# RetNet attention and a SiLU MLP on one core: k and q of three more units transposed by DMA, and the w_out slices converted later

## The chip, the cores and the metric

The kernel runs on one core of one Trainium2 chip. The metric is the device time of one execution in microseconds; less is better. The time of the kernel before is the median of three runs.

## The reference

```python
# q, k, v: (B=4, H=8, S=768, D=64); w_in: (512, 2048); w_out: (2048, 512)
gamma = 1.0 - 2.0 ** (-5.0 - arange(H));  scale = 1.0 / sqrt(D)
for t in range(S):                                  # per batch and head
    state = gamma * state + outer(k[t], v[t])       # (D, D)
    y[t] = scale * (q[t] @ state)
x = y.transpose(0, 2, 1, 3).reshape(3072, 512)      # (B*S, H*D)
h = x @ w_in
out = (h * (1 / (1 + exp(-h)))) @ w_out             # (3072, 512)
```

The weights reach the kernel as 64-bit numbers, two 32-bit words for each element. The output is 32-bit.

## The kernel before, in words

**Chunks and units.** The 768 tokens of each batch are cut into 6 chunks (`NC`) of 128 tokens (`C`). A unit is one chunk of one batch, all 8 heads: 24 units, numbered with the batch running fastest, so that unit 14 is chunk 3, batch 2. The recurrence over tokens is replaced by matmuls within a chunk (scores of q and k times a decay mask) and a state carried from chunk to chunk.

**Precision.** The large products are done in three parts: an operand is split into a high part, a remainder and a mixed part, and the sum of the part products stands for the full precision. So one 512-wide product takes 12 matmuls: 8 into the PSUM bank `ha` (parts 0 and 1) and 4 into the bank `hb` (part 2).

**Phase 1** makes g = silu(x w_in) block by block. `product_in(c, f)` is the block of chunk c (4 batches x 128 tokens = 512 columns) and slice f (128 of the 2048 columns of w_in, `NF` = 16 slices). Its 12 matmuls are at L650. ScalarE copies `ha` out (L660), VectorE subtracts `hb` (L665, kept in `taken_out`), ScalarE applies silu (L670), and the block is stored to DRAM by a DMA on the SyncE queue (L676), one product later. `ha` and `hb` come from three PSUM banks taken in turn (`turn`, L370), which the transposes of k use as well. Blocks of g on chip have three buffers (`hpool`).

**Phase 2** reads g back (L689), splits it (L715 on ScalarE, L717 and L718 on VectorE) and multiplies by w_out (L967, L975); the outputs leave at L984 to L996.

**Visits.** Attention is laid between the products of phase 1. `visit(m)` does, for unit m, the transposes of k and q; for unit m-1, the state sums (L452) and the scores (L462) with their mask and state update on VectorE; for unit m-2, the output y (L501). Its matmuls stand between those of two products. Unit 14 is visited behind product (1,15), units 15, 16 and 17 behind (2,9), (2,11) and (2,13), and from then on one unit behind every fourth product of chunks 3 and 4: (3,1), (3,5) and so on.

**Two ways to transpose.** `FAR` = 17 parts them.

- Units under `FAR`: `stage_t` does 8 transposes on TensorE (L436), four of k into a bank of `turn` and four of q into bank `q`, and two copies on ScalarE take them out (L438).
- Units from `FAR` on: `part_t` copies k and q on GpSimd into two planes of 16 bits (L412), `turn_t` transposes the planes by DMA on the SyncE queue (L419), and `join_t` joins them again on ScalarE (L426). The copies are issued in the visit, the transposing DMAs one product later, the joins in the third product, well before the scores of that unit, which stand in the next visit.

**Slices of the weights.** A slice of w_in or w_out is loaded two takes ahead (`wf`, two buffers). Each `take_w` converts one slice from 64-bit words to 32-bit: one instruction on ScalarE (L196) and six on VectorE: L199, L202, L206, L209, L212, L217. The slices of w_out, 16 of them, go to DRAM again, from the buffer `cw`, of which there is one. In chunk 5 `w_out(f)` reads them back behind product (5, f) and splits them: L120 and L126 on ScalarE, L123 and L128 on VectorE.

**What sets the order.** TensorE's order is the order of the program. On the other engines a scheduler places the instructions, with rules laid over it: `queue(i)` puts what is issued under it right behind instruction i on its engine, `behind_copy` and `behind_next` hold work that goes right behind L660 and L665 of the next product. A list of products, `steps`, is walked from first to last; `takes` lists the products that a slice is converted behind:

```python
takes += [(0, NF - 2), (2, half), (2, half + 2), (2, half + 4)]
takes += [(3, f) for f in (0, 3, 7, 11, 14)]
takes += [(4, f) for f in (3, 7, 11, 14)]
takes += [(5, f) for f in (2, 5, 8)]
```

These sixteen entries (`NF` = 16, `half` = 8) are those of w_out; the earlier ones are those of w_in. A visit that is hung to a product stands in the dictionary `behind`.

**Buffers.** Tiles live in pools by tag: `kf`, `qf`, `vf` for loaded k, q and v (3, 2 and 3 buffers), `kt` (2) and `qt` (3) for transposed tiles, `cw` (1) for a converted slice. `late_y(b)` reads back four tiles of chunk 2 that had been parked in DRAM, into `kt` for even b and `qt` for odd b.

Of the kernel before, what the change touches and what calls it, by code (L numbers as in the profile page):

```python
# [13 lines left out]
FP32 = mybir.dt.float32  # L14
FP32R = mybir.dt.float32r
U32 = mybir.dt.uint32
U16 = mybir.dt.uint16
# [16 lines left out]
def kernel(  # L34
# [28 lines left out]
    nc = tc.nc  # L63
    B, H, S, D = q.shape
    DM, DF = moe_w_in.shape
    C = 128
    NC = S // C
    HP = H // 2
    KIN = DM // 128
    NF = DF // 128  # L70
# [10 lines left out]
    def pool(name, bufs, **kw):  # L81
        return ctx.enter_context(tc.tile_pool(name=name, bufs=bufs, **kw))
# [6 lines left out]
    one = pool("one", 1)  # L89
    hpool = pool("hpool", 3)  # L90
    stage = pool("stage", 2)
    conv = pool("conv", 1)
# [45 lines left out]
    units = [(c, b) for c in range(NC) for b in range(B)]  # L138
    kqv = {"k": {}, "q": {}, "v": {}}
    EARLY = 2 * B  # L140

    FAR = 4 * B + 1
    early = {}

    def load(name, n):
        if n >= len(units):
            return
        c, b = units[n]
        src = {"k": k, "q": q, "v": v}[name]
        if n < EARLY:  # L150

            if n not in early:
                early[n] = wpool.tile([128, 3, H, D], FP32, tag=f"w{4 + n}", name=f"kqv_{n}")
            t = early[n][:, "kqv".index(name)]
        else:
            t = ld.tile([128, H, D], FP32, tag=f"{name}f", name=f"{name}f_{n}",
                        bufs=2 if name == "q" else 3)
        nc.sync.dma_start(out=t, in_=src[b, :, ds(c * C, C)].rearrange("h t d -> t h d"))
        kqv[name][n] = t
# [87 lines left out]
    def queue(ins):  # L247

        return ExitStack() if written[0] or ins is None else tc.issue_after(ins)
# [104 lines left out]
    xt, kt, qt, am = {}, {}, {}, {}  # L354
    behind_next, behind_copy, half_split = [], [], []
    taken_out, copied, masked, fenced = [], [], [], []
# [25 lines left out]
    def scale_k(n):  # L382
        if 0 <= n < len(units):
            t = kqv["k"][n]
            if units[n][0] == NC - 1:
                t = t[:D]
            if 2 * B + 1 < n < 3 * B + 2:

                def half(heads):
                    for h in heads:  # L390
                        nc.scalar.activation(out=t[:, h, :], in_=t[:, h, :], func=AF.Copy,
                                             scale=gk[:, units[n][0], h : h + 1])

                half(range(H // 2))
                behind_copy.append(lambda: half(range(H // 2, H)))
                return
            g = gk[: t.shape[0], units[n][0], :].unsqueeze(2).to_broadcast([t.shape[0], H, D])
            nc.vector.tensor_tensor(out=t, in0=t, in1=g, op=ALU.mult)
# [5 lines left out]

    planes, turned = {}, {}

    def part_t(n):

        for name, (p, tag, bufs) in (("q", (ld, "kf", 3)), ("k", (one, "kt", 2))):
            src = kqv[name].pop(n) if name == "q" else kqv[name][n]  # L410
            t = p.tile([128, 2 * H * D], U16, tag=tag, name=f"{name}p_{n}", bufs=bufs)
            nc.gpsimd.tensor_copy(out=t.rearrange("p (w h d) -> p w h d", w=2, h=H),  # L412
                                  in_=src.bitcast(U16).rearrange("p h (d w) -> p w h d", w=2))
            planes[name, n] = t

    def turn_t(n):
        for name, (p, tag, bufs) in (("q", (ld, "qf", 2)), ("k", (one, "qt", 3))):
            t = p.tile([128, 2 * HP, C], U16, tag=tag, name=f"{name}w_{n}", bufs=bufs)
            nc.sync.dma_start_transpose(out=t, in_=planes.pop((name, n)))  # L419
            turned[name, n] = t  # L420

    def join_t(name, n):

        to, bufs = (qt, 3) if name == "q" else (kt, 2)
        to[n] = one.tile([128, HP, C], FP32, tag=f"{name}t", name=f"{name}t_{n}", bufs=bufs)
        nc.scalar.copy(out=to[n].bitcast(U16).rearrange("p a (t w) -> p w a t", w=2),  # L426
                       in_=turned.pop((name, n)).rearrange("p (w a) t -> p w a t", w=2))

    def stage_t(n):

        for name, to, bufs, src, tp in (
                ("kt", kt, 2, kqv["k"][n], turn(f"kp_{n}")),
                ("qt", qt, 3, kqv["q"].pop(n), banks("q", f"qp_{n}", 1)[:, 0])):
            tp = tp.rearrange("p (a t) -> p a t", a=HP)
            for a in range(HP):
                nc.tensor.transpose(tp[:, a, :], src[:, 2 * a : 2 * a + 2, :], ident)  # L436
            to[n] = one.tile([128, HP, C], FP32, tag=name, name=f"{name}_{n}", bufs=bufs)
            evac[:] = [nc.scalar.copy(out=to[n], in_=tp).ins]  # L438
# [88 lines left out]
    def finish_y(n, yp):  # L527
        list(steps_y(n, yp))
# [52 lines left out]
    y_late = {}  # L581

    def late_y(b):
        tag = ("kt", "qt")[b % 2]
        y_late[b] = one.tile([128, KIN, C], FP32, tag=tag, name=f"yr_{b}", bufs=2 + b % 2)
        nc.sync.dma_start(out=y_late[b], in_=y_dram[b])

    def late_x(b):
# [9 lines left out]
    def halves(m):  # L598

        first, mid, last = (0 <= m - i < len(units) for i in range(3))  # L600
        if first and m < FAR:
            stage_t(m)
        if last:
            scores, states_with, yp = stage_y(m - 2)
            scores()
            states_with(0)
        yield
        if mid:
            sc, sums = score_tile(m - 1)
            stage_s(m - 1, sums)  # L610
            stage_a(m - 1, sc)
            if 1 < m <= 3 * B + 1 and units[m - 1][1] == 0:
                next_chunk()

            with queue(taken_out[0]) if m > 3 * B + 1 else ExitStack():
                finish_a(m - 1, sc, sums)
            scale_q(m - 1)
            if m > 3 * B + 1 and units[m - 1][1] == B - 1:

                behind_copy.append(next_chunk)  # L620
        if first and m < FAR:
            scale_k(m)
        if last:
            states_with(1)
            finish_y(m - 2, yp)

        if FAR <= m < len(units):
            with queue(fenced[0]):
                part_t(m)
        for name in "kqv":  # L630
            for n in (m + 1, m + 2):
                if n >= EARLY and n == (m + 1 if name == "v" or n > FAR else m + 2):
                    load(name, n)
        if EARLY + 2 <= m < 3 * B + 2:
            with queue(masked[0]):
                end_w()
                if m != 3 * B:
                    begin_w()


    pending = []

    def product_in(c, f):
# [168 lines left out]
    def KA(n):  # L812
        t = kqv["k"][n]
        for h in range(H):
# [73 lines left out]
    half = NF // 2  # L888
# [7 lines left out]
    steps = pairs + three + rest + last + groups  # L896
    takes = [(1, 5)] + [(0, f) for f in range(6, half)]
    takes += [(2, half - 4), (2, half - 2)]
    takes += [(0, half), (0, half + 3), (1, half + 1), (1, half + 3)]
    takes += [(0, NF - 2), (2, half), (2, half + 2), (2, half + 4)]  # L900
    takes += [(3, f) for f in (0, 3, 7, 11, 14)]
    takes += [(4, f) for f in (3, 7, 11, 14)]
    takes += [(5, f) for f in (2, 5, 8)]
    behind = {x: lambda: next(half_visits) for x in pairs[:-1]}
    behind[pairs[-1]] = lambda: [visit(3 * B + 1), behind_next.append(end_w)]
    at = ([(1, NF - 1)] + [(2, f) for f in range(NF - 7, NF - 2, 2)] +
          [(c, 4 * i + 1) for c in range(3, NC - 1) for i in range(B)])
    for i, x in enumerate(at):
# [4 lines left out]
    behind[1, NF - 1] = lambda: [late_x(3), visit(EARLY + 6)]  # L913


    far = {steps.index(x): EARLY + 6 + i for i, x in enumerate(at)
           if FAR <= EARLY + 6 + i < len(units)}
    for n, (c, f) in enumerate(steps):
        if n - 2 in far:
            behind_next.append(lambda m=far[n - 2]: scale_k(m))  # L920
        if n - 3 in far:
            behind_copy.append(lambda m=far[n - 3]: [join_t(name, m) for name in "qk"])
        product_in(c, f)
        put_g(1)
        store_w()
        if (c, f) in takes:
            take_w(taken_out[0], n < len(pairs + three))
        behind.get((c, f), lambda: None)()
        if n - 1 in far:
            turn_t(far[n - 1])  # L930
        if c == NC - 1:
            if f == 0:
                for i in range(W_READ):
                    get_w(i)
            if f < NF - 4:
                w_out(f)
            if f >= NF - 6:
                if f == NF - 6:
                    for n in range(G_AHEAD):
                        get(n)  # L940
                if f >= NF - S_AHEAD:
                    split(f - NF + S_AHEAD)
    put_g(0)

    for c in range(NC):
# [9 lines left out]
        for f in range(NF):  # L955
            n = c * NF + f
# [3 lines left out]
            t = ready[n]  # L960
# [17 lines left out]
        for b in range(B):  # L978
            oa, ob = acc[b]
            o = one.tile([128, DM], FP32, tag=("kt", "qt")[b % 2], name=f"o_{c}_{b}",  # L980
                         bufs=(2, 3)[b % 2])
# [8 lines left out]
            n = 2 if b == B - 1 else 1  # L990
# [36 lines left out]
```

## Time and profile before

| | before |
|---|---|
| median of three runs | 621.68 us (620.67, 621.68, 622.66) |
| profiled execution | 619.42 us, its span 617.6 us |
| granted TensorE clock, mean | 1.000 |
| VectorE busy | 422.9 us |
| ScalarE busy | 313.0 us |
| GpSimd busy | 22.6 us |
| DMA | 107.31 MB, mean 174 GB/s |

Busy time is what the engine's instructions occupy, and overlapping instructions make it longer than what they hold the engine for; so for TensorE the chain of waits is the better measure. In the names of engines, PE is TensorE, DVE VectorE, ACT ScalarE, POOL GpSimd and SP SyncE. `L650` is line 650 of the kernel.

One wait on the page is peculiar to this kernel: `POOL token L377`. It comes from `fence`, a tiny memset on GpSimd by which half of the y matmuls of a visit are held until the other half is done.

### The profile page before, as it was taken

The numbers are of one execution on the slowest core, as the hardware profiler recorded it, in microseconds if no ns is written. First come the engines' busy times: TensorE is split into PE (matmuls) and PEld (weight loads), VectorE is DVE, ScalarE is ACT, GpSimd is POOL, SyncE is SP. The second block draws the span as 40 slices with busy tenths as digits, with TensorE's granted clock in tenths as the row PEclk, the third lists the DMA queues.
The fourth block names the chain that finished last, engine by engine and source line by source line (L and its number), as shares of the span: only waits on it lengthen the run. The fifth ranks groups of instructions, "written<-read, shape, count | busy, mean of one in ns | idle before, by whom it ended". The sixth has DMA issues, their size and how long they took to land.

```text
span 617.6 us, 13494 instructions
## 1 busy us (share of the span) xinstructions
PE 603.8 (98%) x5384; PEld 497.5 (81%) x5384; DVE 422.9 (68%) x731; ACT 313.0 (51%) x595; POOL 22.6 (4%) x79
## 2 busy tenths in 40 slices
PE   6899999999999999999999999999999999999997
PEld 5777887888888888888788888888888888888886
DVE  4998889899789877676699773635545453654631
ACT  6678896676654667766587732312221221412311
POOL 3000000000001111120000000000000000000000
PEclk9999999999999999999999999999999999999999
DMA  9989896464677999989767542533524433442301
GB/s 191 225 203 228 243 240 200 157 198 157 222 177 208 259 255 239 259 223 282 255 230 248 203 139 68 171 102 100 173 69 134 140 103 102 141 132 89 116 1 68
DMA packets 137999, 107.31 MB, mean 174 GB/s; under 512 B 94801, under 2 KB 103249, under 8 KB 137937
## 3 DMA queue, kind: packets, MB, share of 16 engines
q1 hardware_dynamic: 135056, 101.21, 57.5%
q10 hardware_dynamic: 2880, 5.24, 2.3%
q8 instruction: 42, 0.69, 0.5%
q14 instruction: 21, 0.16, 0.1%
HBM read 66.06 MB, written 36.70 MB: 166 GB/s over the span
## 4 chain that ended last, share of the span: by engine, by line
PE 84%; DVE 0%; DVEq 0%; issue 0%; POOLq 0%
PE ha L650 25%; PE o L967 21%; PE oa L967 14%; PE hb L650 12%; PE ob L967 7%; PE y L501 2%; PE sc L462 1%; PE sc L452 1%; PE o L975 0%; PE oa L975 0%; PE qp L436 0%; PE kp L436 0%; PE ob L975 0%; DVE o L993 0%; DVEq L1022 0%
## 5 line engine op out<-in xcount | busy, mean ns | idle before, releaser
L650 PE MATMUL ha<-xt,wi 128*128 128x512 f32 x768 | 193.8, 394 | 1.3 <-ACT xt L557 0.7
L650 PEld LDWEIGHTS ha<-xt,wi 128*128 128x128 f32 x768 | 141.9, 188 | 33.6 <-ACT wi L126 1.2
L967 PE MATMUL o<-wo,gs 128*128 128x512 f32 x564 | 143.2, 389 | 0.0
L717 DVE TENSOR_TENSOR gs<-gr,gs 128x512 fp32r<-128x512 f32 x96 | 62.1, 685 | 90.3 <-ACT gs L715 90.3
L967 PEld LDWEIGHTS o<-wo,gs 128*128 128x128 f32 x564 | 105.9, 188 | 21.9
L715 ACT ACTIVATE gs<-gr 128x512 fp32r<-128x512 f32 x96 | 53.6, 621 | 134.2 <-issue 131.8
L967 PE MATMUL oa<-wo,gs 128*128 128x512 f32 x376 | 115.8, 389 | 0.0
L650 PE MATMUL hb<-xt,wi 128*128 128x512 f32 x384 | 102.9, 390 | 0.0
L665 DVE TENSOR_TENSOR g<-g,hb 128x512 f32<-128x512 f32 x96 | 65.6, 683 | 42.0 <-ACT g L660 26.3
L650 PEld LDWEIGHTS hb<-xt,wi 128*128 128x128 f32 x384 | 71.8, 188 | 15.5 <-DVE g L665 0.2
L670 ACT ACTIVATE g<-g 128x512 f32<-128x512 f32 x96 | 60.3, 628 | 47.1 <-DVE g L665 47.1
L967 PEld LDWEIGHTS oa<-wo,gs 128*128 128x128 f32 x376 | 70.6, 188 | 14.7
L967 PE MATMUL ob<-wo,gs 128*128 128x512 f32 x188 | 73.7, 392 | 0.0
L660 ACT ACTIVATE g<-ha 128x512 f32<-128x512 f32 x96 | 57.0, 594 | 31.9 <-PE ha L650 15.1
L718 DVE SCALAR_TENSOR_TENSOR gs<-gs 128x512 fp32r<-128x512 f32 x96 | 62.0, 683 | 0.0
L967 PEld LDWEIGHTS ob<-wo,gs 128*128 128x128 f32 x188 | 35.3, 188 | 8.7 <-DVE o L985 1.6
L196 ACT ACTIVATE ca<-wf 128x512 f32<-128x512 f32 x32 | 21.4, 668 | 6.0 <-DVE cw L217 5.5
L212 DVE SCALAR_TENSOR_TENSOR ca<-wf,ca 128x512 f32<-128x512 uint32 x32 | 22.7, 710 | 0.5
L984 ACT ACTIVATE o<-o 128x512 f32<-128x512 f32 x10 | 6.0, 600 | 33.4 <-PE o L967 33.0
L206 DVE SCALAR_TENSOR_TENSOR cs<-ca,cs 128x512 uint32<-128x512 uint32 x32 | 22.1, 691 | 0.9
L501 PE MATMUL y<-qt,mid 64*64 64x64 f32 x384 | 20.2, 224 | 1.0 <-POOL token L377 1.0
L470 DVE TENSOR_TENSOR am<-sc,decay 128x512 f32<-128x512 f32 x24 | 16.5, 687 | 6.6 <-PE sc L462 6.5
(93 smaller groups left out, 562.0 us busy)
## 6 DMA issues: line engine op xcount, KB each, us to landing
gd<-g SPq DMA_DIRECT2D x96, 256.0 KB, 3.1
gr<-gd SPq DMA_DIRECT2D x96, 256.0 KB, 2.7
wf<-in_moe_w_out_dram SPq DMA_DIRECT2D x16, 512.0 KB, 4.2
out_dram<-o ACTq DMA_DIRECT2D x20, 256.0 KB, 2.1
wf<-in_moe_w_in_dram SPq DMA_DIRECT2D x16, 256.0 KB, 4.2
wf<-in_moe_w_in_dram SPq DMA_DIRECT2D x32, 128.0 KB, 4.0
kf<-in_k_dram SPq DMA_DIRECT2D x16, 256.0 KB, 5.1
qf<-in_q_dram SPq DMA_DIRECT2D x16, 256.0 KB, 4.0
```

What stands on the lines that cost most here:

```text
L196: nc.scalar.activation(out=a.bitcast(FP32), in_=hi.bitcast(FP32), func=AF.Abs, scale=65536.0)
L206: nc.vector.scalar_tensor_tensor(out=s, in0=a, scalar=3, in1=s, op0=ALU.logical_shift_left, op1=ALU.bitwise_or)
L212: nc.vector.scalar_tensor_tensor(out=p.bitcast(FP32), in0=lo, scalar=2.0 ** -52, in1=p.bitcast(FP32), op0=ALU.mult, op1=ALU.mult)
L501: i = nc.tensor.matmul(yp[ts(e, D), o, a, :], lhsT=lhsT, rhs=rhs, start=(e, o) not in started, stop=True, skip_group_check=True).ins
L650: nc.tensor.matmul(hb if i == 2 else ha, lhsT=w_sb[f][:, i, ts(kk, 128)], rhs=xt[c][:, i, kk, :], start=kk == 0 and i != 1, stop=kk == KIN ...
L660: copied[:] = [nc.scalar.activation(out=hs, in_=ha, func=AF.Copy, scale=ONE_E).ins]
L665: taken_out[:] = [nc.vector.tensor_tensor(out=hs, in0=hs, in1=hb, op=ALU.subtract).ins]
L670: nc.scalar.activation(out=hs, in_=hs, func=AF.Silu)
L715: nc.scalar.activation(out=t[:, 0, :], in_=g, func=AF.Copy, scale=HALF)
L717: nc.vector.tensor_tensor(out=t[:, 1, :], in0=g, in1=high, op=ALU.subtract)
L718: nc.vector.scalar_tensor_tensor(out=t[:, 2, :], in0=t[:, 1, :].bitcast(FP32), scalar=-1.0 / EPS, in1=high, op0=ALU.mult, op1=ALU.add)
L967: nc.tensor.matmul(o, lhsT=g, rhs=wo[f][:, i, :], start=f == 0 and i != 1, stop=f == NF - 1 and i != 0)
```

## The change

`FAR` goes from 17 to 14: k and q of units 14, 15 and 16 go the way of the DMA as well, and TensorE no longer transposes them. A second bound, `LATER` = 17, keeps what units from 17 on do as it was. What belongs to it:

- Unit 14 is split long ahead: its `part_t` is tied to L665 of product (2,3), its transposes follow behind (2,5), its join behind L660 of (2,8). Unit 15 is split in the visit of 14, turned behind (2,8) and joined at (2,10); unit 16 is split in the visit of 15, turned behind (2,10) and joined at (2,12).
- Loads: k and q of 15 and q of 16 are loaded at hand-set places, and k of 16 into the buffer `cw`.
- `late_y` of odd batches uses `cw` instead of `qt`, whose buffers now carry planes.
- As `cw` is used by these, no slice of w_out can be converted there before the end of chunk 2. The takes at (0,14), (2,8), (2,10) and (2,12) fall away, and (2,15), one more in chunk 3, one more in chunk 4 and one more in chunk 5 come instead.

```diff
-    FAR = 4 * B + 1
+    FAR = 3 * B + 2
+    LATER = 4 * B + 1
...
+        if n == LATER - 1 and name == "k":
+            t = conv.tile([128, H, D], FP32, tag="cw", name=f"kf_{n}")
+            nc.sync.dma_start(out=t, in_=src[b, :, ds(c * C, C)].rearrange("h t d -> t h d"))
+            kqv[name][n] = t
+            return
...
-    def part_t(n):
+    def part_t(n, after=None):
...
+            if after is not None:
+                tc.add_manual_dep(i, after.name, mybir.DependencyInfo(
+                    mybir.DependencyClass.Sync, mybir.DependencyReason.DATA), reason="later")
...
-        tag = ("kt", "qt")[b % 2]
-        y_late[b] = one.tile([128, KIN, C], FP32, tag=tag, name=f"yr_{b}", bufs=2 + b % 2)
+        p, tag, bufs = ((one, "kt", 2), (conv, "cw", 1))[b % 2]
+        y_late[b] = p.tile([128, KIN, C], FP32, tag=tag, name=f"yr_{b}", bufs=bufs)
...
-        if first and m < FAR:
+        if first and m < LATER:
             scale_k(m)
...
-        if FAR <= m < len(units):
+        n = m if m >= LATER else m + 1
+        if FAR < n < len(units) and (m < LATER - 1 or m >= LATER):
             with queue(fenced[0]):
-                part_t(m)
+                part_t(n)
...
-    takes += [(0, NF - 2), (2, half), (2, half + 2), (2, half + 4)]
-    takes += [(3, f) for f in (0, 3, 7, 11, 14)]
-    takes += [(4, f) for f in (3, 7, 11, 14)]
-    takes += [(5, f) for f in (2, 5, 8)]
+    takes += [(2, NF - 1)]
+    takes += [(3, f) for f in (0, 3, 6, 8, 11, 14)]
+    takes += [(4, f) for f in (0, 3, 7, 11, 14)]
+    takes += [(5, f) for f in (1, 3, 5, 8)]
...
+    first_far = steps.index((2, 3))
+    parts = {first_far: FAR}
+    turns_at = {first_far + 2: FAR, far[FAR] + 1: FAR + 1, far[FAR + 1] + 1: FAR + 2}
+    joins_at = {far[m] + 1: m for m in range(FAR, LATER)}
+    for m in range(LATER, len(units)):
+        turns_at[far[m] + 1], joins_at[far[m] + 3] = m, m
+    scales_at = {far[m] + 2: m for m in range(LATER, len(units))}
+    loads_at = {first_far + 4: [("k", FAR + 1), ("q", FAR + 1)], far[FAR] + 1: [("q", FAR + 2)]}
```

More of the change, by code (lines that the diff above doesn't have):

```diff
@@ L411, in part_t @@
             t = p.tile([128, 2 * H * D], U16, tag=tag, name=f"{name}p_{n}", bufs=bufs)
-            nc.gpsimd.tensor_copy(out=t.rearrange("p (w h d) -> p w h d", w=2, h=H),
-                                  in_=src.bitcast(U16).rearrange("p h (d w) -> p w h d", w=2))
+            i = nc.gpsimd.tensor_copy(
+                out=t.rearrange("p (w h d) -> p w h d", w=2, h=H),
+                in_=src.bitcast(U16).rearrange("p h (d w) -> p w h d", w=2)).ins
+            if after is not None:
+                tc.add_manual_dep(i, after.name, mybir.DependencyInfo(
+                    mybir.DependencyClass.Sync, mybir.DependencyReason.DATA), reason="later")
             planes[name, n] = t
@@ L625, in halves @@
             finish_y(m - 2, yp)
-        if FAR <= m < len(units):
+        n = m if m >= LATER else m + 1
+        if FAR < n < len(units) and (m < LATER - 1 or m >= LATER):
             with queue(fenced[0]):
-                part_t(m)
+                part_t(n)
         for name in "kqv":
             for n in (m + 1, m + 2):
-                if n >= EARLY and n == (m + 1 if name == "v" or n > FAR else m + 2):
+                if (n, name) not in apart and n >= EARLY and n == (
+                        m + 1 if name == "v" or n >= LATER else m + 2):
                     load(name, n)
@@ L638, in halves @@
                     begin_w()
+    apart = [(FAR + 1, "k"), (FAR + 1, "q"), (FAR + 2, "q")]
     pending = []
@@ L913 @@
     behind[1, NF - 1] = lambda: [late_x(3), visit(EARLY + 6)]
-    far = {steps.index(x): EARLY + 6 + i for i, x in enumerate(at)
-           if FAR <= EARLY + 6 + i < len(units)}
-    for n, (c, f) in enumerate(steps):
[L919 to L922, printed above, removed]
+    far = {m: steps.index(x) for m, x in enumerate(at, EARLY + 6)}
+    first_far = steps.index((2, 3))
[6 more added lines that the diff above has]
+    loads_at = {first_far + 4: [("k", FAR + 1), ("q", FAR + 1)], far[FAR] + 1: [("q", FAR + 2)]}
+    for n, (c, f) in enumerate(steps):
+        if n in scales_at:
+            behind_next.append(lambda m=scales_at[n]: scale_k(m))
+        if n in joins_at:
+            behind_copy.append(lambda m=joins_at[n]: [join_t(name, m) for name in "qk"])
+        if n in parts:
+            behind_next.append(lambda m=parts[n]: part_t(m, taken_out[0]))
         product_in(c, f)
@@ L928 @@
         behind.get((c, f), lambda: None)()
-        if n - 1 in far:
-            turn_t(far[n - 1])
+        if n in turns_at:
+            turn_t(turns_at[n])
+        for name, m in loads_at.get(n, ()):
+            load(name, m)
         if c == NC - 1:
```

## The prediction

> **What bounds the kernel now.** First the busy times and the slices of the page, then the chain that ended last around the transposes, then the busy time by stretch of chunk 5, and last the order of time on DVE there.
>
> ```profile
> PE 603.8 (98%) x5384; PEld 497.5 (81%) x5384; DVE 422.9 (68%) x731; ACT 313.0 (51%) x595; POOL 22.6 (4%) x79
> PE   6899999999999999999999999999999999999997
> ```
>
> PE is at 90% or more from the third slice (about 31 us) to the last but one. From 100 us to 600 us it is busy in every 25 us stretch but for 0.3 us at 302 us, so a microsecond of PE work removed there is a microsecond of the end, as long as nothing else takes its place. How long PE work really holds the engine must be read from the chain, because matmuls overlap:
>
> ```profile
> 169.41 0.91 PE hb L650 x4
> 170.32 0.44 PE kp L436 x4
> 170.76 0.44 PE qp L436 x4
> 171.19 0.86 PE y L501 x48
> 172.05 0.47 PE sc L452 x32
> 172.52 0.47 PE sc L462 x32
> 172.99 0.23 PE y L501 x16
> 173.22 2.04 PE ha L650 x8
> ...
> 196.02 0.86 PE y L501 x48
> 196.88 0.47 PE sc L452 x32
> 197.34 0.47 PE sc L462 x32
> 197.81 0.23 PE y L501 x16
> 198.04 2.04 PE ha L650 x8
> ```
>
> Columns: start, length, engine, tile, line. The visit of unit 14 (170.32 to 173.22) lasts 2.90 us, those of 15 and 16 (178.89, 187.45) the same; the visit of 17 (196.02 to 198.04), whose k and q already come by DMA, lasts 2.02. The difference is exactly the eight L436 transposes, 0.44 + 0.44.
>
> DVE, with 68%, looks free, but not where the slices of w_out are finished:
>
> ```profile
> 305.00:325.00 20.00, 20.00 (x90) 16.55 (x89) 19.26 (x35) 16.41 (x31) 0.00 (x0) 1.00 0.64 216
> 325.00:340.00 15.00, 15.00 (x68) 12.26 (x67) 15.00 (x28) 11.11 (x21) 0.00 (x0) 1.00 0.71 241
> 340.00:352.00 12.00, 12.00 (x54) 9.84 (x54) 8.21 (x14) 8.53 (x17) 0.00 (x0) 1.00 0.67 230
> ```
>
> Columns: stretch and its length, then busy time and instructions of PE, its weight loads, DVE, ACT and POOL, the granted clock, the DMA share and GB/s. From 307 to 340 us, chunk 5, DVE never rests. PE is still full, but by little:
>
> ```profile
> 336.99 0.69 DVE L665 TENSOR_TENSOR g<-g,hb 128x512 f32<-128x512 f32 x1
> 337.59 0.69 DVE L212 SCALAR_TENSOR_TENSOR ca<-wf,ca 128x512 f32<-128x512 uint32 x1
> 338.19 0.69 DVE L123 SCALAR_TENSOR_TENSOR wol<-wr,wo 128x512 f32<-128x512 f32 x1
> 338.80 0.69 DVE L217 TENSOR_TENSOR cw<-cs,ca 128x512 f32<-128x512 f32 x1
> 339.40 0.69 DVE L128 SCALAR_TENSOR_TENSOR wo<-wo,wol 128x512 fp32r<-128x512 f32 x1
> 340.00 0.69 DVE L665 TENSOR_TENSOR g<-g,hb 128x512 f32<-128x512 f32 x1
> ```
>
> Each L665 empties the bank hb of one product. The starts are 0.60 us apart, which is what one such instruction really takes of DVE (0.34 for L199, L202 and L209: starts 334.18, 334.52, 334.85). The last line is product (5,10). Its hb was complete when the next ha began, 338.27 in the chain, so DVE is 1.73 us late. Three banks turn and a product uses two, so the bank is wanted by ha two products on, one step of 2.72 us later. With 0.68 us for L665 itself, its start may be at most 2.04 us late before PE stands.
>
> **What the skill says.** "TensorE: Matmul & The Clock Gate", section "Part 4: PE-mode transpose", gives some 275 ns for one transpose in a kernel. The trace has 271 to 273 ns of latency for these, but in a row they hold PE 0.11 us each (four in 0.44), so I price with the chain. "SBUF — State Buffer", section "Who interferes with whom", says that a DVE instruction with two SBUF inputs and a GpSimd instruction that reads SBUF lock each other out. The trace agrees: L212 and L217 last 1.41 us at 197.65 and 199.09, beside the L412 copies, and 0.69 elsewhere. "Advanced Engine Details and Errata", section "X-Bar Transpose (TRN2)", calls transposing DMAs as fast as plain ones. The landing agrees (3.1 to 5.7 us, middle 3.7), but each also holds the SP queue for about 1.3 us, where a plain one takes 0.3 to 0.5.
>
> **The change, part by part.**
>
> 1. Removed on PE: three visits times 0.44 + 0.44, 2.63 us. The built order of PE differs in nothing else. All of it is on the path.
>
> 2. Added on POOL: two L412 copies per unit, 1.07 + 1.19 us, three times. POOL is idle 96%. Beside them DVE loses some 1.4 us per unit (two instructions of 1.41 instead of 0.69). For units 15 and 16 that is free, for the w_out slices leave this stretch, each worth 3 x 0.60 + 3 x 0.34 = 2.8 us of DVE. Unit 14 is split after the L665 of product (2,3), at about 121 us, beside w_in slices. Running the built DVE order against the 2.72 us steps with 1.4 to 1.6 us added, L665 gets at most 1.8 us late, under 2.04: nothing.
>
> 3. Added on SP: six transposes, 1.3 us of issue each, with the stores of g queued behind them (and behind the waits for POOL and for the joins, which free their buffers). A g store 3 us later still lands before its buffer is wanted three products (8 us) on. Nothing.
>
> 4. ACT: two copies out of PSUM (0.58 each) become two joins, L426, 1.36 each, starts 1.25 apart. Who waits is L462 of the next visit. Without the transposes, that of unit 15 starts its L462 at 186.8; L660 of (2,10) starts at 182.2, the joins end at 185.3. Unit 16 is the tight one, since the four L350 (1.27 us in all) come first: L660 of (2,12) at 189.85, L350 to 191.65, joins to 194.25, while L462 falls due at 194.5. The copies still arrive in time: kw of 16 is issued when the join of 15 frees its buffer, 185.4, and lands by 190. Price 0, bounds 0 and 0.4 us.
>
> 5. w_out slices moved: four of the sixteen leave 150 to 200 us. Three go into chunks 3 and 4 (two slices in one 13.1 us period at (2,15)/(3,0), (3,6)/(3,8), (3,14)/(4,0)), the fourth into chunk 5. In chunks 3 and 4 DVE has the room (18 to 20 us busy of 25). DMA has less: share 0.91 to 0.96, and a slice brings 512 + 256 KB, 2.2 us at the 354 to 376 GB/s seen at 288 to 294 us. A late transpose holds ACT at the join. In the trace joins end 0.65 us (unit 17) to 1.5 us before their L462, so up to about a microsecond is swallowed. Price 0, bounds 0 and 0.5 us at each of the three.
>
> 6. Chunk 5: the slices end with products 1, 3, 5 and 8 instead of 2, 5 and 8, and the built order of DVE between two L665 follows. Six others (3 long, 3 short) and the L665 take 3.42 us, four take 3.00, one takes 1.20, seven take 4.02. Every group is compared with a step of 2.72. For before, from the lag 0.39 us of product 1 (314.14 against 313.75), groups of 3.00, 3.42, 3.00, 1.20, 4.02, 3.00, 1.20, 4.02, 3.00 give lags 0.67, 1.37, 1.65, 0.13, 1.43, 1.71, 0.19, 1.49, 1.77. The trace has 0.67, 1.37, 1.65, 0.12, 1.42, 1.70, 0.17, 1.44, 1.73, so the count holds. After has 3.42, 3.00, 3.42, 3.00, 3.42, 3.00, 1.20, 4.02, 3.00 for products 2 to 10: lags 1.09, 1.37, 2.07, 2.35, 3.05, 3.33, 1.81, 3.11, 3.39. The largest passes 2.04 by 1.35 us, and PE must stand that long in all, between products 6 and 12. The splits of g that stood among these groups before (L717, L718) come after product 11 and catch up there.
>
> Sum: 621.68 - 2.63 + 1.35 = 620.40, and 0.1 for the handover at some five new waits: **620.5 us**.
>
> **Rivals.**
>
> A. The queue of DVE doesn't bind, for PE has more room than I count (0.5). Then the whole 2.63 us is kept: 619.05. For it: no PE wait in chunk 5 is listed before, at lags up to 1.73. Against it: bank and step are plain in the order, and ha after product 10 begins 0.05 us late even now (341.04, 2.77 after 338.27).
>
> B. More waits than the one of DVE: joins late behind the crowded DMA at the three doubled periods and unit 16 (0.2 to 0.4 us each), and in chunk 5 L660 waiting for the store of g three products back, which happened already (2.43 us of ACT, at 336.7). About 1.3 us more: 621.8. For it: DMA share 0.96. Against it: slack of 1.15 us and more at most joins.
>
> C. Slower. Transposes of five units (15, 16, 18, 20, 22) come late by about 0.8 us beyond the slack, for every transfer stands in the one SP queue: 620.5 + 4.0 = 624.5. Against it: six transposes of the same kind run every 40 us already without a PE wait.
>
> **How the numbers follow.** Forecast 0.50, A 0.23, B 0.20, C 0.07. Faster by over 0.3% means under 619.8: A and a little of the forecast's lower side, 0.28. Slower by over 0.3%, over 623.5: C and the end of B, 0.08. The rest is 0.64. The range reaches from just under A, 618.8, to B with both its bounds, 622.8.
>
> **What would show it.** In the profile after: visits of units 14 to 16 of 2.02 us each (step 1). No PE wait near 194 us (step 4) and none by ACT L426 in chunks 3 and 4 (step 5). In chunk 5 PE waits on DVE L665, together about 1.4 us, and L665 start lags near 2.04 at products 5 to 10 (step 6). No such wait means A; waits of L462 on ACT mean B or C. The forecast is wrong if PE has under 0.7 us of idle in chunk 5, or over 2.5 us in all between 165 and 352 us.

## The result and the profile after

| | before | after |
|---|---|---|
| median of six runs each | 621.01 us | 627.17 us |
| lowest, highest | 618.99, 622.66 | 624.94, 627.57 |
| ratio | | 1.0092, 95% interval 1.0067 to 1.0118 |
| span of the profiled execution | 617.6 us | 625.4 us |

The changed kernel is slower by 0.9%, where 620.5 us had been forecast, with 622.8 as the upper end.

The busy times and the slices of PE, from the page of the changed kernel:

```profile
PE 601.7 (96%) x5360; PEld 491.9 (79%) x5360; DVE 425.7 (68%) x731; ACT 316.9 (51%) x595; POOL 29.3 (5%) x85
PE   5798999999999999999999999999999999999997
```

PE has lost its 24 transposes (5360 instructions for 5384, 601.7 us for 603.8). The page says little more, since almost every slice of PE still reads 9. So each kernel's TensorE timeline was read for the start of the first `ha` matmul of each of the 96 products, and the starts of after were compared with those of before. This shows place by place where time goes (after minus before, us; the column at the right is what was added since the line above):

| start of product | after - before | added |
|---|---|---|
| (1,4) | 0.02 | |
| (0,6) | 2.23 | +2.2, all but 0.2 of it in one step, at (0,5) |
| (2,8) | 1.34 | -0.87, visit of unit 14 |
| (2,10) | 0.46 | -0.88, visit of unit 15 |
| (2,14) | 0.00 | -0.46, visit of unit 16 |
| (3,6) | 1.69 | +1.69 |
| (3,14) | 4.41 | +2.72 |
| (5,0) | 6.06 | +1.65, of it 1.55 at (4,4) |
| (5,15) | 7.68 | +1.62, chunk 5 |

So the transposes' gain is there, 2.2 of 2.63 us. It is eaten more than four times over, by three losses.

**The first loss, 2.1 us, before anything is transposed.** The SyncE queue of before and after, from the timeline (start, length, line, output and input). Before:

```profile
73.91 0.68 SPq L546 DMA_DIRECT2D yd<-ys  x1
74.65 0.42 SPq L676 DMA_DIRECT2D gd<-g  x1
76.38 0.38 SPq L158 DMA_DIRECT2D qf<-in_q_dram  x1
78.20 0.32 SPq L676 DMA_DIRECT2D gd<-g  x1
```

After:

```profile
74.94 0.42 SPq L689 DMA_DIRECT2D gd<-g  x1
79.93 0.32 SPq L596 DMA_DIRECT2D yr<-yd  x1
80.34 0.39 SPq L164 DMA_DIRECT2D qf<-in_q_dram  x1
80.82 0.54 SPq L689 DMA_DIRECT2D gd<-g  x1
```

A read-back, `yr`, stands where none stood before, at 79.93. It is `late_y(1)`. The program asks for it behind (0,14), 80 us later, but its new buffer, `cw`, is free at this time, and the scheduler put it at the first place at which its buffer and its source allow it: right behind the store that it reads. The queue stood 4.6 us for that store to land, with the load of q and the store of g behind it. The blocks of g share their three buffers with that store, so L673 (the copy of `ha`, L660 in before) of product (1,4) started at 86.25, where in before it started at 84.05, and PE lost 2.06 us at (0,5).

**The second loss, 6.1 us in chunks 3 and 4.** What PE waited for between 175 and 300 us in after (engine and line, releaser, us in total, times, longest); the same question to the kernel before has no line at all:

```profile
PE hb L663 <- ACT g L673: 2.9, 4, 1.2
PE sc L472 <- ACT kt L436: 1.4, 2, 1.0
PE y L511 <- DVE xt L570: 0.3, 1, 0.3
```

L472 (the scores) waits for the join L436, and `hb` for a bank that L673 copies out on ScalarE. What held ScalarE up is not the same at every place.

At (3,6) and (3,14), where 0.71 and 2.06 us of the table were lost, it was DMA. The two engines around unit 20, ahead of (3,14), first ScalarE and then TensorE:

```profile
249.93 0.60 ACT L673 ACTIVATE g<-ha 128x512 f32<-128x512 f32 x1 [2.15 <-DMA gd<-g]
251.43 1.38 ACT L436 COPY qt<-qw 128x1024 uint16<-128x1024 uint16 x1 [0.90 <-DMA qw<-qp]
```

```profile
250.58 1.20 PE L663 MATMUL hb<-xt,wi 128*128 128x512 f32 x4 [0.58 <-ACT g L673]
254.04 0.69 PE L472 MATMUL sc<-qt,kt 64*64 64x64 f32 x32 [0.96 <-ACT kt L436]
```

In the brackets stands how long the engine was idle and for what: ScalarE stood for a store of g and then for a transpose, and PE stood for ScalarE. The SyncE queue ahead of this:

```profile
238.28 0.90 SPq L164 DMA_DIRECT2D vf<-in_v_dram  x1
241.87 0.34 SPq L188 DMA_DIRECT2D wf<-in_moe_w_out_dram  x1
242.56 0.34 SPq L286 DMA_DIRECT2D wod<-cw  x1
242.99 0.38 SPq L164 DMA_DIRECT2D kf<-in_k_dram  x1
243.49 0.86 SPq L689 DMA_DIRECT2D gd<-g  x1
244.46 2.57 SPq L429 DMA_TRANSPOSE qw<-qp  x1
247.44 2.15 SPq L429 DMA_TRANSPOSE kw<-kp  x1
```

For 2.7 us nothing is issued. The load of a slice (`wf`, 512 KB) waits for L218, which frees its buffer, and L218 ended at 241.81. Then 1.25 MB go out within 1.6 us (512, 256, 256 and 256 KB), and the transposes stand behind them. The busy share of the DMA engines over these 10 us, 238 to 248, in 40 tenths:

```profile
DMA  9899989999899983110875899969999999999999
```

They work off what they have, run dry for a microsecond (3110, at 241.8 to 242.8 us), and then are full. The transpose of q, issued at 244.46, is joined at 251.43. The same five issues (slice load, slice store, k, g, transpose of q) take 2.6 us from the first to the last here, and 5.9 us in before, with two more between them:

```profile
234.63 0.53 SPq L182 DMA_DIRECT2D wf<-in_moe_w_out_dram  x1
235.25 0.38 SPq L280 DMA_DIRECT2D wod<-cw  x1
...
236.80 1.52 SPq L158 DMA_DIRECT2D kf<-in_k_dram  x1
238.44 1.94 SPq L676 DMA_DIRECT2D gd<-g  x1
240.48 2.26 SPq L419 DMA_TRANSPOSE qw<-qp  x1
```

At (3,4), (3,12) and (4,4), where 0.98, 0.65 and 1.55 us were lost, no join stood ahead. There ScalarE stood at L202, the first step of the next slice (L196 in before), until VectorE had finished the slice ahead of it with L223. L202 writes the buffer `ca`, of which there is one, L223 reads it last, and in ScalarE's order L673 stands behind L202. Ahead of (4,4), VectorE, ScalarE and TensorE:

```profile
271.72 0.69 DVE L223 TENSOR_TENSOR cw<-cs,ca 128x512 f32<-128x512 f32 x1
272.45 0.67 ACT L202 ACTIVATE ca<-wf 128x512 f32<-128x512 f32 x1 [1.16 <-DVE cw L223]
273.50 0.59 ACT L673 ACTIVATE g<-ha 128x512 f32<-128x512 f32 x1
274.14 1.20 PE L663 MATMUL hb<-xt,wi 128*128 128x512 f32 x4 [1.25 <-ACT g L673]
```

L202 stood 3.91, 1.40 and 1.16 us at these three places, each time for the slice that ends a doubled period. In before L196 stands for VectorE nowhere between 205 and 300 us. So a doubled period costs in two ways, each about half of the 6.1 us: stores and transposes that land late (2.8 us), and a step of the next slice that stands ahead of a copy which PE needs (3.2 us).

**The third loss, 1.6 us in chunk 5,** is the one forecast. The starts of L678 of products 2 to 10 lie 3.41, 3.01, 3.41, 3.00, 3.41, 3.01, 1.20, 4.01 and 3.01 us after those ahead of them; the count had 3.42, 3.00, 3.42, 3.00, 3.42, 3.00, 1.20, 4.02, 3.00. PE stands for it:

```profile
337.18 2.11 PE L663 MATMUL ha<-xt,wi 128*128 128x512 f32 x8 [0.38 <-DVE g L678]
```

### The profile page after: what moved, and what is told of

Read it like the earlier page. It is cut to its first block, busy times and chain, and to the rows that moved or that the text cites. A ratio compares the mean times of both kernels' runs of the same rounds, so it can differ in the third digit from the quotient of the medians.

```text
span 625.4 us, 13466 instructions
## 1 busy us (share of the span) xinstructions
PE 601.7 (96%) x5360; PEld 491.9 (79%) x5360; DVE 425.7 (68%) x731; ACT 316.9 (51%) x595; POOL 29.3 (5%) x85
## 4 chain that ended last, share of the span: by engine, by line
PE 68%; DVE 5%; DMA 4%; ACT 3%; issue 2%; SPq 1%; POOL 1%; DVEq 0%; POOLq 0%
PE o L991 20%; PE ha L663 16%; PE oa L991 14%; PE hb L663 8%; PE ob L991 7%; DMA qw<-qp 3%; PE y L511 1%; DVE g L678 1%; DMA wod<-cw 1%; ACT qt L436 1%; ACT kt L436 1%; DMA qf<-in_q_dram 1%; DVE ca L218 1%; PE sc L472 1%; DVE ca L208 0%
## 5 line engine op out<-in xcount | busy, mean ns | idle before, releaser
L678 DVE TENSOR_TENSOR g<-g,hb 128x512 f32<-128x512 f32 x96 | 65.6, 684 | 42.3 <-ACT g L673 27.2
L673 ACT ACTIVATE g<-ha 128x512 f32<-128x512 f32 x96 | 56.9, 593 | 32.9 <-PE ha L663 16.1
L212 DVE SCALAR_TENSOR_TENSOR cs<-ca,cs 128x512 uint32<-128x512 uint32 x32 | 24.2, 758 | 0.8
L202 ACT ACTIVATE ca<-wf 128x512 f32<-128x512 f32 x32 | 21.3, 665 | 6.5 <-DVE cw L223 6.5
L218 DVE SCALAR_TENSOR_TENSOR ca<-wf,ca 128x512 f32<-128x512 uint32 x32 | 22.0, 688 | 0.5
L480 DVE TENSOR_TENSOR am<-sc,decay 128x512 f32<-128x512 f32 x24 | 16.5, 686 | 6.7 <-PE sc L472 6.7
```

What stands on the lines that cost most here:

```text
L202: nc.scalar.activation(out=a.bitcast(FP32), in_=hi.bitcast(FP32), func=AF.Abs, scale=65536.0)
L212: nc.vector.scalar_tensor_tensor(out=s, in0=a, scalar=3, in1=s, op0=ALU.logical_shift_left, op1=ALU.bitwise_or)
L218: nc.vector.scalar_tensor_tensor(out=p.bitcast(FP32), in0=lo, scalar=2.0 ** -52, in1=p.bitcast(FP32), op0=ALU.mult, op1=ALU.mult)
L673: copied[:] = [nc.scalar.activation(out=hs, in_=ha, func=AF.Copy, scale=ONE_E).ins]
L678: taken_out[:] = [nc.vector.tensor_tensor(out=hs, in0=hs, in1=hb, op=ALU.subtract).ins]
```

## The experiments

They ran on other chips, where the median of the kernel before was 622.5 to 623.7 us and where the stretch ahead of product (0,6) was 2.3 to 6.5 us longer than in the profile of before. So beside the ratios the starts of products are used, counted from (0,6), each against the profile of before, in us. A is from (0,6) to (2,14), the visits of units 14 to 16; B from (2,14) to (5,0); C from (5,0) to (5,15). A letter rests on one profiled execution. In A, e1 and e9 to e11, which change nothing there, read 0.0 to -0.3; in B, after and e6, whose programs do the same there, are 1.3 apart. The ratios rest on 4 to 22 executions of each kernel and hold the stretch ahead of (0,6) as well.

| run | ratio to before, 95% interval | A | B | C |
|---|---|---|---|---|
| after | 1.0092, 1.0067 to 1.0118 | -2.2 | +6.1 | +1.6 |
| e1_late_takes | 1.0080, 1.0048 to 1.0112 | 0.0 | +4.1 | +1.8 |
| e5_early_takes | 1.0014, 0.9999 to 1.0028 | -0.3 | +2.2 | 0.0 |
| e6_wl | 1.0059, 1.0040 to 1.0079 | -2.6 | +4.8 | +1.6 |
| e7_first_slice | 1.0060, 1.0040 to 1.0079 | -2.3 | +5.6 | +1.6 |
| e8_g_on_act | 1.0130, 1.0096 to 1.0165 | -2.2 | +8.5 | +2.3 |
| e9_bytes | 1.0063, 1.0037 to 1.0089 | -0.2 | +2.2 | 0.0 |
| e10_dve | 1.0022, 1.0001 to 1.0043 | -0.2 | +0.6 | 0.0 |
| e11_bytes_dve | 1.0079, 1.0040 to 1.0118 | -0.3 | +5.4 | 0.0 |
| e12_unit14 | 0.9997, 0.9979 to 1.0015 | -1.2 | +1.2 | 0.0 |
| e13_chunk5 | 1.0069, 1.0049 to 1.0088 | -2.3 | +5.1 | 0.0 |
| e14_half_g | 1.0039, 1.0024 to 1.0054 | -2.3 | +2.6 | +1.6 |
| e15_early_half_g | 1.0017, 0.9996 to 1.0037 | -0.2 | +1.5 | 0.0 |
| e16_held_loads | 1.0066, 1.0043 to 1.0089 | -2.6 | +8.3 | 0.0 |
| e17_unit14_held | 0.9976, 0.9958 to 0.9993 | -1.0 | 0.0 | 0.0 |
| e18_wl_held | 1.0043, 1.0023 to 1.0062 | -2.2 | +3.3 | +2.1 |

### The takes and the transposes, each alone

e1 is the kernel before with the four lines of `takes` of after. e5 is the changed kernel with those of before, and

```diff
-            t = conv.tile([128, H, D], FP32, tag="cw", name=f"kf_{n}")
+            t = conv.tile([128, H, D], FP32, tag="wl", name=f"kf_{n}")
...
-        p, tag, bufs = ((one, "kt", 2), (conv, "cw", 1))[b % 2]
+        p, tag, bufs = ((one, "kt", 2), (conv, "wl", 1))[b % 2]
```

e6 has the same two lines and keeps the late takes. e7 is e6 with `(2, NF - 1)` in `takes` replaced by `(2, half + 4)`.

> The kernel before, with only the list of takes of the change: the slices of w_out are converted from the end of chunk 2 on, all of units 0 to 16 are still transposed on TensorE. Theory (three losses: a load hoisted in the SyncE queue before 90 us, 2.1 us; crowded slices in chunks 3 and 4, 5.9 us; the VectorE queue in chunk 5, 1.5 us): the second and third appear here without the change's gain, 621.0 + 5.9 + 1.5 = 628.4 us, with PE losing time at the same three places, behind products (3,1), (3,9) and (4,1). Rival (the six new transposes and their loads upset the SyncE queue for good): 621 to 622.5.

> The changed kernel with the takes of the kernel before; k of unit 16 and the read-back tiles of odd batches live in the buffer wl, which is idle between the last slice of w_in and chunk 5, so that cw is free for slices. Theory: only the transposes' gain is left, 621.0 - 2.6 + 0.4 (unit 16) = 618.8 us, no PE wait in chunks 3 and 4 beyond those of before. Rival (the transposes themselves do the harm): 624 or more.

> The changed kernel with its own takes, but wl in place of cw for k of unit 16 and the read-back tiles of odd batches. As wl is still in use by w_in slices at 80 us, the read-back of batch 1 cannot be issued there any more. Theory: the loss of 2.1 us between products (1,4) and (0,5) is gone and all else stays, 627.2 - 2.1 = 625.1 us. Rival (that loss was a chance of the DMA in one execution): 627.2.

> As the one before (wl in place of cw), and the first slice of w_out is converted behind (2,12) instead of (2,15), so that it no longer stands one product ahead of the slice at (3,0). Theory (two slices in one visit's period are what costs, place by place): the 1.7 us lost between (3,1) and (3,6) are gone, the losses after (3,9) and (4,1) stay: 625.1 - 1.7 = 623.4 us. Rival (what costs is the number of bytes and slices in chunks 3 and 4 as a whole, or one product's delay feeding the next): under 0.5 us better than the run with wl alone, 624.6 or more; or all the losses go together, 619.5 to 621.

e1 loses 4.1 us in B and 1.8 in C without one new transpose, and in B at the places named (0.9 by (3,6), 2.5 by (3,14), 0.7 at (4,4)). So most of the second loss and all of the third belong to the takes.

e6 has no step at (0,5), nor has any other run with `wl`, and by the ratios it is faster than after by about 0.33% of 621, 2.0 us (the two intervals overlap). The first loss is the read-back.

e5 misses its number: 0.9 us over before, not 2.2 under it. The early takes pay in another coin: 1.3 us are lost again at (2,12) and (2,14), and 1.9 at (3,2). Busy times of the stretch 175 to 205 us (PE, its weight loads, DVE, ACT, POOL), first of after, then of e5:

```profile
175.00:205.00 30.00, 29.66 (x486) 24.55 (x486) 21.00 (x36) 19.52 (x30) 5.63 (x8) 1.00 0.99 203
```

```profile
175.00:205.00 30.00, 28.34 (x484) 23.02 (x477) 29.62 (x51) 19.48 (x30) 7.06 (x9) 1.00 0.99 226
```

With slices and GpSimd copies in one stretch DVE is busy 29.62 of 30 us (27.36 in before). The DMA share is 0.99, but so it is in after, which loses nothing there but 0.4 us at unit 16.

e7 takes the first pair of slices apart, and what the pair had cost went: L202 ahead of (3,4) no longer stands for VectorE (3.8 us in e6), and (3,4) and (3,6) lose nothing. But 1.3 us came at (3,2) instead, where the slice at (2,12) now puts its load and store ahead of the transposes of unit 17, and the join came late. So a single slice costs too where it stands badly.

### Bytes, VectorE time, or the queue

e9 and e11 add to before, in the loop over `steps`,

```diff
+        if (c, f) in [(3, 0), (3, 9), (4, 1)]:
+            more = dram.tile([128, 3, DM], FP32, tag=f"more{n}", name=f"more_{n}")
+            i = nc.sync.dma_start(out=more, in_=decay.rearrange("p j a d -> p (j a d)")
+                                  .unsqueeze(1).to_broadcast([128, 3, DM])).ins
+            tc.add_manual_dep(i, taken_out[0].name, ...)
```

and e10 and e11

```diff
+        if (c, f) in [(2, 15), (3, 8), (4, 0)]:
+            with queue(taken_out[0]):
+                t = conv.tile([128, DM], FP32, tag="wl", name=f"idle_{n}")
+                for _ in range(5):
+                    nc.vector.tensor_tensor(out=t, in0=..., in1=..., op=ALU.mult)
```

e8 is e6 with the stores of g of chunks 3 and 4 issued by `nc.scalar`.

> The changed kernel with wl in place of cw, and the stores of g of chunks 3 and 4 issued by ScalarE, behind the silu that makes them, instead of standing in the SyncE queue ahead of the transposes. Theory Q (transposes come late because they stand in one queue behind stores and loads that wait for VectorE and ScalarE): most of the 4.7 us that the run with wl alone loses on PE between (2,15) and (5,0) are gone, under 2 us left. Theory B (the transposes are issued in time enough but land late, because the bytes ahead of them fill the DMA engines): 4 us or more are still lost, and landings stay near 5 to 7 us.

> The kernel before, and 768 KB more written to DRAM, the bytes of one slice's load and store, at three places only, behind (3,0), (3,9) and (4,1), as one transfer each that waits for L665 there; no VectorE work is added. Theory B: PE loses 0.7 to 1.7 us at each of the three, 2 to 5 us in all, as with the late takes alone (4.0 us). Theories Q and D (VectorE): 0 to 0.6 us in all.

> The kernel before, and five VectorE instructions of 128x512, 3.0 us, more behind (2,15), (3,8) and (4,0), a slice's worth of VectorE time without its transfers; their result is not used. Theory D (the second slice of a period makes VectorE late with the mask, and with that the slice's and the visit's followers): 2 to 4 us lost between (2,15) and (5,0). Theory B: 0 to 0.6 us.

> The kernel before with both additions, the 768 KB and the 3.0 us of VectorE at the three places. If only their meeting hurts (VectorE late, and so loads and stores bunched just ahead of the transposes): here 3 us or more, with the two single runs under 1 us each. If the losses add: the sum of the two single runs. If the cause is something else, such as the one buffer cw or the order that slices give to the SyncE queue: under 1 us here as well.

In these profiles bytes alone lose 2.2 us, VectorE time alone 0.6, both together 5.4, where the late takes alone (e1) lost 4.1. That the two hurt more than their sum is not shown: over all executions the losses are 0.63, 0.22 and 0.79%. What the traces do show is that they hurt in different ways. With bytes alone PE has three waits between 175 and 300 us, all for late joins (L426). With VectorE time alone it has one, ahead of (3,4), behind an L196 that stood 2.7 us for VectorE's L217. (The transfer of e9 waits for L665, so it holds up the queue for a while too.)

Taking the stores of g out of the SyncE queue did not help: B went from 4.8 to 8.5, and transposes landed up to 9.9 us after their issue, against 6.2 at most in e6. As ScalarE spends 0.33 us on each store that it issues, this run does not say what the place of the stores in the queue is worth.

### Half of the bytes of g, chunk 5, and one unit alone

e13 is e6 with takes at (2,12) and (2,15) and those of chunk 5 as before, (5,2), (5,5), (5,8). e14 (on e6) and e15 (on e5) store `g[:, :NT // 2]` for the blocks named. For these blocks the second phase reads the stored half twice, so that half of their g is left out of the result. e12 is the kernel before with unit 14 alone sent by DMA, and the read-backs of odd batches in `wl`.

> The changed kernel with wl in place of cw, with slices behind both (2,12) and (2,15), and in chunk 5 those of before, (5,2), (5,5), (5,8). Theory of step 6 (the fourth slice in chunk 5 makes L665 late): no PE wait on VectorE in chunk 5, 0.0 to 0.2 us lost there instead of 1.5; what is lost between (2,12) and (5,0) stays at 4 us or more. Rival (chunk 5 is late because of the state in which chunk 4 hands over): 1 us or more is lost in chunk 5 still.

> The changed kernel with wl in place of cw, its own late takes, and only half the columns of each g block of chunks 3 and 4 stored (128 KB less for each of 32 products; the second phase reads the stored half twice, so that part of the result is left out). Theory B (bytes ahead of the transposes make them late): of the 4.7 us lost between (2,15) and (5,0) under 2 are left. Rival (order of the SyncE queue, waits for VectorE): 3.5 us or more stay.

> The changed kernel with the takes of before and wl in place of cw (the run that lost 3.5 us between (2,10) and (3,2)), with half of each g block left out in the same way from (2,8) to (3,15). Theory B: under 1.5 us of the 3.5 are left, so that the three units' transposes keep most of their 2.63 us. Rival (VectorE, slowed by the copies on GpSimd beside the early slices, is the cause): 2.5 us or more stay lost.

> The kernel before, with unit 14 alone transposed by DMA, long ahead as in the change (behind (2,5), where the DMA engines are busy 0.55 of the time); units 15 and 16 stay on TensorE and the takes are those of before; the read-back tiles of odd batches are in wl. Theory (a transpose costs only where the DMA engines are full): the visit of 14 is 0.88 us shorter and nothing is lost for it, the products from (2,8) on start 0.7 to 0.9 us earlier than before, relative to (0,6). Rival (any transpose of the three brings its own late join or queue): less than 0.4 us is kept at (5,0).

e13 settles the third loss: C is 0.0. e14 falls between its theories: with half of the bytes of 32 blocks gone, 2.6 us of 4.8 are left. e15 goes to the rival: up to (2,14) it loses as much as e5, so there it is not the bytes of g. VectorE fits (busy 29.62 of 30 us in e5, where PE's longest wait ahead of (2,14), 0.9 us, is for L570 on VectorE), but no run took that load away.

e12 gains its 0.88 us at (2,8) and loses 1.14 at (3,2), the scores of unit 17, which is far from unit 14. Its SyncE queue there:

```profile
202.43 0.33 SPq L183 DMA_DIRECT2D wf<-in_moe_w_out_dram  x1
203.15 0.33 SPq L281 DMA_DIRECT2D wod<-cw  x1
203.57 0.38 SPq L159 DMA_DIRECT2D kf<-in_k_dram  x1
204.05 0.88 SPq L684 DMA_DIRECT2D gd<-g  x1
205.02 2.29 SPq L424 DMA_TRANSPOSE qw<-qp  x1
```

The same picture again, an empty queue from 199.6 to 202.43 and then everything at once. ScalarE's join stood for the transpose until 211.28, 1.86 us.

### The load held behind the transposes

`load_w` gets an instruction to wait for, and for some takes it is called three products later:

```diff
+        if n in waiting:
+            load_w(waiting.pop(n), copied[0])
         if (c, f) in takes:
+            hold[0] = [n + 3] if (c, f) in [(2, 12), (3, 0)] else None
```

e17 is e12 with this, e18 is e6 with it at (3,0), (3,8), (4,0), and e16 is e13 with it at the same three.

> As the run with unit 14 alone by DMA, and the loads issued from the takes at (2,12) and (3,0) held behind the transposes in the same way. Theory: the 1.14 us lost at (3,2) is gone and the 0.88 us of unit 14 is kept to the end, 0.7 to 0.9 us earlier at (5,0) than before, relative to (0,6). Rival: 0.5 us or more is lost at (3,2) again.

> As the run with wl alone, but the load of a slice that is issued from the takes at (3,0), (3,8) and (4,0) waits for L673 three products on, so that in the SyncE queue it stands behind the transposes and no longer ahead of them. Nothing else is moved, bytes and VectorE work are the same. Theory (the queue stands at this load, then everything is issued at once ahead of the transposes): of the 4.8 us lost between (2,15) and (5,0) under 2 us are left. Rival (bytes and VectorE time as such, wherever they stand): 3.5 us or more stay lost.

> As the run with slices behind (2,12) and (2,15) and chunk 5 as before, with the loads issued from the takes at (3,0), (3,8) and (4,0) held behind the transposes. Theory: of the 5.0 us lost between (2,12) and (5,0) under 2 us are left, and as the three units save 2.0 us by (2,12), the kernel is as fast as before or up to 1.5 us faster. Rival: 4 us or more stay lost, 2 us or more slower than before.

e17's SyncE queue, and then the join on ScalarE:

```profile
203.28 0.32 SPq L286 DMA_DIRECT2D wod<-cw  x1
203.70 0.39 SPq L159 DMA_DIRECT2D kf<-in_k_dram  x1
204.17 1.52 SPq L429 DMA_TRANSPOSE qw<-qp  x1
205.79 1.28 SPq L429 DMA_TRANSPOSE kw<-kp  x1
...
208.29 0.38 SPq L183 DMA_DIRECT2D wf<-in_moe_w_out_dram  x1
```

```profile
209.31 1.36 ACT L436 COPY qt<-qw 128x1024 uint16<-128x1024 uint16 x1 [0.46 <-DMA qw<-qp]
```

The 512 KB of `wf` now follow the transposes, the join starts 2 us earlier than in e12, the step at (3,2) is 0.00 and unit 14's gain stays: 622.2 us against 623.65, ratio 0.9976. It is the one kernel here whose whole interval lies under before, by little; the profile accounts for 1.0 of the 1.45 us.

e18 gains where the pattern was clearest, from (3,10) to (3,14) (2.8 us lost without the hold, 0.6 with it), but 3.3 of 4.8 us stay. PE's waits in chunks 3 and 4 of e18, and ScalarE ahead of the longest:

```profile
PE hb L668 <- ACT g L678: 2.1, 3, 1.2
```

```profile
273.74 0.67 ACT L205 ACTIVATE ca<-wf 128x512 f32<-128x512 f32 x1 [1.15 <-DVE cw L226]
```

No wait for a join is left. The three that are left lie ahead of (3,4), (3,12) and (4,4), steps of 0.87, 0.58 and 1.53 us, and each follows an L205 (L202 in after) that stood for VectorE to give back `ca`: 3.78, 1.40 and 1.15 us. The hold took away the one kind of loss and left the other.

e16 loses more than e13. Its largest step, 4.5 us at (3,4) and (3,5), is the same wait for `ca`, 4.31 us of ScalarE, made longer by one for the one buffer `cw`:

```profile
217.50 0.69 DVE L226 TENSOR_TENSOR cw<-cs,ca 128x512 f32<-128x512 f32 x1 [2.00 <-DMA wod<-cw]
```

Two slices follow each other by one product there ((2,15), (3,0)), and the first one's store took 6.0 us to land, from 211.49.

## Why the prediction was wrong

Step 1 (24 transposes less, 2.63 us) was right: the visits of units 14 and 15 gave 0.87 and 0.88.

Step 2 (GpSimd's copies, "free" for units 15 and 16) held for VectorE's slower instructions but overlooked a wait. GpSimd's L418 reads k while VectorE's L404 is to scale it in place, and GpSimd itself was late: the load of q of unit 16 had been issued behind the transposes of 15. The chain at unit 16 (a piece each, "issue" left out):

```profile
178.68 3.47 DMA qf<-in_q_dram
...
182.30 0.82 POOL qp L418
183.28 1.06 POOL kp L418
...
184.36 0.69 DVE kf L404
185.05 0.60 DVE am L480
...
187.51 0.61 DVE xt L570
...
188.26 0.93 PE y L511 x48
```

VectorE stood 2.92 us at L404, with the mask L480 and the x of the last unit, L570, behind it, and PE lost 0.4 us of that visit's gain. Step 4 had this size as its upper bound, with ScalarE as the cause.

Step 3 (SyncE: "Nothing") failed as well: it counted the six transposes and left `late_y` out, whose change of buffer let a read-back rise by 80 us to where the queue had no room: 2.1 us.

Step 5 failed most: the moved slices in chunks 3 and 4 were priced 0, at most 0.5 us at each doubled period, and cost 1.69, 2.72 and 1.65. VectorE's room and the DMA share were each weighed by their mean over 25 us, and the only path to PE that the step looked at was a late transpose. The runs showed two paths, both of waits for a buffer. In a doubled period VectorE frees the slice's buffer `wf` late, the SyncE queue stands at the load, and then 1.25 MB go out at once, just ahead of the transposes: about 2.8 us at (3,6) and (3,14). That VectorE frees `ca` late too, and ScalarE stands for it ahead of the copy of `ha`, the step did not look at: about 3.2 us at (3,4), (3,12) and (4,4). For the first, e12 against e17 shows that in one place the position of that one load is the whole of it, and e18 that holding the loads removes the waits for joins in chunks 3 and 4. For the second, e7 shows that it goes at (3,4) when the pair is taken apart, and e10 that VectorE time alone brings it there; that e18 is left with it is read from its trace. No run moved L202 behind L673.

Step 6 was right: 1.35 us forecast, 1.6 measured, in the products named, and gone in e13.

Rival C, with a chance of 0.07, had named one of the two: transposes late beyond their slack, five of them, 4.0 us in all. Its time, 624.5, was still short of 627.17, since it had neither the wait for `ca` nor the read-back. What was set against it, that transposes ran there already without a wait, was the weak point: they ran with 0.65 to 1.5 us of slack, which step 5 counted as room and which the bunched transfers used up.

Open: which part of e5's loss up to (2,14) is VectorE's and why it loses 1.9 us at (3,2); why half of the bytes of g is worth 2.2 us in e14, and which of the two ways they act on; and what of B is left if L202 stands behind L673 and a second `ca` and `cw` are there.

## What to carry to other kernels

A mean share leaves out the order: where an in-order queue carries loads that wait for buffers and transfers that others wait for, list the issues ahead of the urgent one and ask of each what it waits for. Giving a tile another buffer moves its load too, to the first place at which that buffer is free, so look up the built order of the DMA queue as well as those of the compute engines. The same holds for an engine that only prepares: its next step, placed early, can stand for a buffer with urgent work behind it, as L202 did. And before a resource is called sufficient, look at how much slack the waits behind it have now: 0.65 to 1.5 us were used up here by a bunch of transfers.

## What the runs showed of the hardware

The time from issue to landing of a transposing DMA differed with what was issued just before. That of q of unit 17 took 4.6 us in before, where the slice's load had gone out 3.3 us ahead of it, 6.2 us in e12, where it had gone out 2.6 us ahead, and 5.1 us in e17, where it was held back. The Trainium skill ("Advanced Engine Details and Errata", section "X-Bar Transpose (TRN2)") calls such transfers as fast as plain ones. In before the trace comes near that, as the store of g issued just ahead took 4.2 us; in e12 it does not, with 4.7 us for the store and 6.2 for the transpose. VectorE beside GpSimd's copies was again twice as slow as alone, L212 1.41 us at 238.49 in after, where it took 0.69 at 205.80, which fits the skill's "SBUF — State Buffer", section "Who interferes with whom": a VectorE instruction with two inputs in SBUF contends with a GpSimd instruction that reads SBUF.
